# A transform table in four parts, a later first transform, and eleven weight groups fetched ahead, in a one-core convolution and spectral-mixing kernel

## The chip, the cores and the metric

The kernel runs on one core of a Trainium2 chip. The metric is the device time of one execution in microseconds (us), the median of several runs. A core has TensorE (PE; PEld is its weight load), VectorE (DVE), ScalarE (ACT), GpSimd (POOL) and SyncE (SP). Here GpSimd issues the loads of inputs and weights, and SyncE the stores of the output.

## What is computed

A causal convolution of 7 taps along the sequence, with one set of softmaxed taps for each of 8 heads of 24 channels. Its result goes through a Fourier transform along the sequence; the lowest 64 modes are multiplied by a complex 192 x 192 matrix each; the inverse transform is added, and a last product with a clamp follows.

```python
# x (8, 3264, 192), weight (8, 7); B, S, D, H, K, group = 8, 3264, 192, 8, 7, 24
w = np.exp(weight - np.max(weight, axis=-1, keepdims=True))
w = w / (np.sum(w, axis=-1, keepdims=True) + 1e-09)
x_unf = x_pad[:, idx, :].reshape(B, S, K, H, group)
x = np.einsum('hk,bskhg->bshg', w, x_unf).reshape(B, S, D)
# w_r, w_i (64, 192, 192), w_ch (192, 192)
X = np.fft.rfft(x, axis=1)
Xr, Xi = (np.real(X[:, :n_modes]), np.imag(X[:, :n_modes]))
Yr = np.einsum('bmd,mde->bme', Xr, w_r) - np.einsum('bmd,mde->bme', Xi, w_i)
Yi = np.einsum('bmd,mde->bme', Xr, w_i) + np.einsum('bmd,mde->bme', Xi, w_r)
Y[:, :n_modes] = Yr + 1j * Yi
u = x + np.fft.irfft(Y, n=S, axis=1)
out = u + np.maximum(u @ w_ch, 0.0)
```

## The kernel before

Every engine runs its instructions in the order in which the program writes them, so the order of the text is the order of each queue.

**Layout.** The 8 batches are taken as 4 pairs (`q`). Of each batch, 26 tiles of 128 rows lie in `xall` (bf16). The pairs are worked off in units `(q, b0, n)` of n double tiles: pair 0 in three units of 3, 4 and 6, the others in two units of 7 and 6, nine in all. `load_unit` (L144 on) loads a unit from memory by GpSimd, one DMA for each of its two batches (L150) and one for the last, shorter tile (L154). `arena` holds, at first, temporary arrays (`turns`, `whole`, the taps, masks and indices), then five buffers for groups of spectral weights, then the outputs. `ct` (312 blocks of 128 x 128) will hold the transposed `xall`; the blocks of the last pair serve as three more weight buffers before that (`late`). `spots` lists the eight buffers, and `wts` says which group lies in which.

**Head.** VectorE and ScalarE clear arrays, GpSimd makes indices (`cidx`, `sidx`, `midx`, L160 to L165), TensorE multiplies zeros (`NIDLE` times, L180). VectorE makes masks (L184), the softmax runs (L186 to L196, the exponential on ScalarE, L189, and a small sine behind it, L190), and the taps are put into `packed` under masks (L204), in two halves of four heads. Copies of 32 rows each, four for each half, make `band` of it: the first half on ScalarE (L212), the second on VectorE (L214).

**The Fourier table.** `ftab` holds cosines and sines for 26 tiles x 64 modes. `table(step, t0, t1)` makes a part of it in six steps: a product (L223), rounding by a large constant (L226), the difference (L228), on VectorE; the sine (L230), the absolute value (L232) and the cosine (L234), on ScalarE. It is made in two parts, of 14 and 12 tiles: the first part's VectorE steps ahead of unit 0, its ScalarE steps behind it; the whole second part behind unit 1.

**Convolution.** `conv_step` (L294 on) does one head and one parity of a unit with matmuls against `band`: lower rows at once, upper rows two steps later. For pair 0 one PSUM tile of two banks holds both parities of a head; there are four such tiles. The result is copied back over `xall`: L331 on ScalarE, L333 on VectorE, by a rule of head and unit. For the other pairs there are eight tiles of one bank, and L339 (ScalarE) and L341 (VectorE) copy.

**Forward transform.** `dft(q, t0, t1)` (L355) multiplies the tiles of `xall` by `ftab` and sums; the first half of a pair's sum is kept in `xacc` (L358, L360), the second is added to it (L362). `xtrans(q)` (L374, L376) transposes the sum into `xt`, with casts on VectorE (L383) and ScalarE (L385). For pair 0, `dft` over 14 tiles stands behind unit 1, and that over the other 12 and `xtrans` behind unit 2. For the other pairs both are done by `dfts` in the middle of a later unit, after head 2. Six filler matmuls (L421) stand behind unit 0.

**Mixing.** Weights come in 16 groups of four modes, each two DMAs of GpSimd (`load_w`, L273): eight groups after unit 3, others as `mix` frees a buffer. `mix(g)` (L495) multiplies a group; `mix_copy` (L508, L510) scales the result into `ymix` on ScalarE, `mix_trans` transposes it, and two copies (L535, L537) put it into `yet`. Between the mixes `some(n)` takes n jobs of a list of 44: four banks of transposed `ftab`, a small job for `wsw`, and 39 banks of eight transposed blocks of `xall` into `ct` (L456, copied by L446 on ScalarE every third time, else by L448 on VectorE). The two PSUM banks of the mix are cleared by VectorE (L439).

**Output.** From the last mixes on, `both` (L565), `full` (L627) and `product` (L696) make 104 output tiles in PSUM; ScalarE clamps (L620), VectorE adds `xall` (L607), SyncE stores.

Of the kernel before, what the change touches and what calls it, by code (L numbers as in the profile page):

```python
# [9 lines left out]
ALU = mybir.AluOpType  # L10
ACT = mybir.ActivationFunctionType
AX = mybir.AxisListType
F32 = mybir.dt.float32
BF16 = mybir.dt.bfloat16
U16 = mybir.dt.uint16
PSUM = bass.MemoryType.PSUM


@with_exitstack
def kernel(  # L20
# [9 lines left out]
    nc = tc.nc  # L30
# [15 lines left out]
    MAGIC = 12582912.0  # L46
    NIDLE = 31
    UNITS0 = ((0, 3), (3, 4), (7, 6))
# [7 lines left out]

    NW = 5
    WGB = 4 * 3 * D
    sb("pad", [64], BF16)
# [27 lines left out]

    late = ct[:, 3 * NT * (NQ - 1):3 * NT * NQ, :].rearrange("p t s -> p (t s)")
    spots = [arena[:, WGB * i:WGB * (i + 1)] for i in range(NW)]
    spots += [late[:, WGB * i:WGB * (i + 1)] for i in range(3)]  # L90
    spots = [a.rearrange("p (m j e) -> p m j e", m=4, j=3) for a in spots]
    wts = [spots[g] if g < NW + 3 else spots[(g - NW - 3) % NW] for g in range(MODES // 4)]

    zwl = spots[NW - 1].rearrange("p m j e -> p (m j e)").rearrange("p (b t d) -> p b t d", t=2, b=B - 2)
    NO = 6
# [20 lines left out]
    wrec = temp(H, F32)  # L116
    wsin = temp(H, F32)
    cidx = temp(PW, F32)
# [24 lines left out]

    def load_unit(q, b0, n):  # L144
        nf = min(n, NB - 1 - b0)
        s0 = NB * q + b0 + 1
        for i in range(2):
            off = ((2 * q + i) * S + 2 * P * b0) * D
            src = bass.AP(tensor=x.tensor, offset=x.offset + off, ap=[[2 * D, P], [2 * P * D, nf], [1, 2 * D]])
            nc.gpsimd.dma_start(out=xin[:, s0:s0 + nf, 2 * D * i:2 * D * (i + 1)], in_=src)  # L150
        if nf < n:
            off = (2 * q * S + 2 * P * (NB - 1)) * D
            src = bass.AP(tensor=x.tensor, offset=x.offset + off, ap=[[2 * D, PL], [S * D, 2], [1, 2 * D]])
            nc.gpsimd.dma_start(out=xin[0:PL, s0 + nf, :].rearrange("p (i c) -> p i c", i=2), in_=src)  # L154
# [3 lines left out]
                                           ap=[[0, P], [KK, H], [1, KK]]))  # L158
    load_unit(*units[0])
    nc.gpsimd.iota(cidx[:, 0:PW], pattern=[[1, PW]], base=0, channel_multiplier=-1,  # L160
                   allow_small_or_imprecise_dtypes=True)
    load_unit(*units[1])
    nc.gpsimd.iota(sidx.rearrange("p (b a) -> p b a", a=2), pattern=[[2 * P, NB], [1, 2]], base=0,
                   channel_multiplier=2, allow_small_or_imprecise_dtypes=True)
    nc.gpsimd.iota(midx, pattern=[[1, MODES]], base=0, channel_multiplier=0,  # L165
                   allow_small_or_imprecise_dtypes=True)
    nc.vector.memset(packed, 0.0)
    nc.vector.memset(xin[:, 0, :], 0.0)
    bandrow = shared[:, 0:H * 2 * BW]
    nc.scalar.copy(out=bandrow[:, H * BW:], in_=packed[:, 0:1].to_broadcast([P, H * BW]))  # L170
    nc.vector.memset(bandrow[:, 0:H * BW], 0.0)
    for g in range(4):
        nc.vector.memset(goff[32 * g:32 * g + 32, :], float(32 * g))
    nc.vector.memset(xin[PL:P, NB:NB * NQ + 1:NB, :], 0.0)
    nc.vector.memset(halfpi[:], math.pi / 2)
# [7 lines left out]
    for k in range(KK // 2 + 1):  # L183
        nc.vector.tensor_scalar(out=masks[:, PW * k:PW * (k + 1)], in0=cidx[:, 0:PW],  # L184
                                scalar1=float(k), scalar2=None, op0=ALU.is_equal)
    nc.vector.reduce_max(out=wmax, in_=wr3, axis=AX.X)  # L186
    nc.vector.tensor_tensor(out=wsub.rearrange("p (h k) -> p h k", h=H), in0=wr3,
                            in1=wmax.unsqueeze(2).to_broadcast([P, H, KK]), op=ALU.subtract)
    nc.scalar.activation(out=wexp, in_=wsub, func=ACT.Exp)  # L189
    nc.scalar.activation(out=wsin, in_=ascale.to_broadcast([P, H]), func=ACT.Sin)  # L190
    we3 = wexp.rearrange("p (h k) -> p h k", h=H)
# [8 lines left out]
    for h0 in (0, H // 2):  # L200
        hs = slice(h0, h0 + H // 2)
        for lag in range(KK):
            k = lag // 2
            nc.vector.copy_predicated(  # L204
                out=pk4[:, hs, lag % 2, :],
                mask=masks[:, PW * k:PW * (k + 1)].unsqueeze(1).to_broadcast([P, H // 2, PW]),
                data=ta3[:, hs, KK - 1 - lag:KK - lag].to_broadcast([P, H // 2, PW]))
        for g in range(4):
            c0 = 1 + 32 * (g % 2)
            dst, srcv = band[32 * g:32 * g + 32, hs, :, c0:c0 + PW], pk4[32 * g:32 * g + 32, hs, :, :]  # L210
            if h0 == 0:
                nc.scalar.copy(out=dst, in_=srcv)  # L212
            else:
                nc.vector.tensor_copy(out=dst, in_=srcv)  # L214
    nc.vector.tensor_scalar(out=sidx, in0=sidx, scalar1=1.0 / S, scalar2=None, op0=ALU.mult)
    tu3 = turns.rearrange("p (t m) -> p t m", t=NT)
    wh3 = whole.rearrange("p (t m) -> p t m", t=NT)

    def table(step, t0, t1):
        n = t1 - t0  # L220
        tu, wh = tu3[:, t0:t1, :], wh3[:, t0:t1, :]
        if step == 0:
            nc.vector.tensor_tensor(out=tu, in0=sidx[:, t0:t1].unsqueeze(2).to_broadcast([P, n, MODES]),  # L223
                                    in1=midx.unsqueeze(1).to_broadcast([P, n, MODES]), op=ALU.mult)
        elif step == 1:
            nc.vector.tensor_scalar(out=wh, in0=tu, scalar1=MAGIC, scalar2=-MAGIC, op0=ALU.add, op1=ALU.add)  # L226
        elif step == 2:
            nc.vector.tensor_tensor(out=tu, in0=tu, in1=wh, op=ALU.subtract)  # L228
        elif step == 3:
            nc.scalar.activation(out=ftab[:, t0:t1, 1:2 * MODES:2], in_=tu, func=ACT.Sin, scale=-TWOPI)  # L230
        elif step == 4:
            nc.scalar.activation(out=wh, in_=tu, func=ACT.Abs)  # L232
        else:
            nc.scalar.activation(out=ftab[:, t0:t1, 0:2 * MODES - 1:2], in_=wh, func=ACT.Sin, scale=-TWOPI,  # L234
                                 bias=halfpi[:, 0:1])

    load_unit(*units[2])
# [63 lines left out]
    def conv_step(u):  # L301
# [26 lines left out]
        if q == 0:  # L328
            srcv = tile0[:, :, 0:2 * GRP * n].rearrange("p a (b i e) -> p a b i e", b=n, i=2)
            if (h < 5 if b0 == 0 else h > 4 if b0 == units[1][1] else h % 2):  # L330
                nc.scalar.copy(out=dst, in_=srcv)  # L331
            else:
                nc.vector.tensor_copy(out=dst, in_=srcv)  # L333
# [52 lines left out]

    p1, p2 = (0, 14), (14, NT)
    todo = []
# [8 lines left out]

    for step in range(3):
        table(step, *p1)
    for k, u in enumerate(units):  # L400
        for h in range(H):
            for a in range(2):
                conv_step((*u, h, a))
            if k > 3 and h == 2:
                if pend:
                    xtrans(pend.pop(0))
                dfts()
        if k == 3:
            for g in range(NW + 3):
                load_w(g)  # L410
        if u[0]:
            todo.append((u[0], 2 * u[1], 2 * (u[1] + u[2])))
            continue

        flush()
        if k == 0:
            for step in range(3, 6):
                table(step, *p1)
            z = free.pop(0)
            for _ in range(6):  # L420
                nc.tensor.matmul(z[:, 0, :], band[:, 0, 0, 0:P], band[:, 0, 0:1, 0:P].to_broadcast([P, 4, P]), start=True,  # L421
                                 stop=True, skip_group_check=True)
            free.append(z)
        elif k == 1:
            for step in range(6):
                table(step, *p2)
            dft(0, *p1)
        else:
            free[:] = open_psum("left", (1, 1, 1, 1)) + open_psum("right", (1, 1, 1, 1))
            dft(0, *p2)  # L430
            xtrans(0)
    flush()
# [5 lines left out]
    for z in zm:  # L438
        nc.vector.memset(z[:, 0:2 * D], 0.0)  # L439
    tbank = [0]  # L440
    ncopy = [0]

# [47 lines left out]
    def mix(g, bank):  # L490
        yp = bank[:, D * (g % 2):D * (g % 2) + D]
        for j in range(3):
            for p4 in range(4):
# [3 lines left out]
                                 tile_position=(0, 32 * p4), skip_group_check=True)  # L497
        if g < NW:
            load_w(g + NW + 3)
        elif g >= NW + 3:  # L500
            load_w(g + NW)

# [132 lines left out]
    for d in range(ND - 2):  # L635
        mix(2 * d, zm[d % 2])
        mix(2 * d + 1, zm[d % 2])
        mix_copy(d, zm[d % 2], 0, 2)

        some(2 if d < 4 else 4)  # L640
        mix_trans(d, 0, 2)
        some(2 if d < 4 else 4 if d < ND - 3 else 8)
    d = ND - 2
# [15 lines left out]
    zw_pair(2, zm[0], zm[1])  # L659
    zw_pair(3, ze[0], ze[1])  # L660
    mix(NG - 1, zm[0])
    mix_copy(d, zm[0], 1, 1)
    both(1, 0, "c", begin=True)
    mix_trans(d, 1, 1)
    both(1, 1, "c")
    for b in range(2):
# [118 lines left out]
```

## Time and profile before

| | us |
|---|---|
| median of 3 runs (lowest, highest) | 176.38 (176.29, 176.39) |
| profiled execution, its own time | 177.44 |
| span of the profiled execution | 175.6 |

The table below gives busy time by stage, in us, from the windows of the profiled execution; the last column is the rate of all DMA.

| stage, us of the span | PE | DVE | ACT | GB/s |
|---|---|---|---|---|
| 0 to 32.3: head and pair 0 | 27.94 | 22.48 | 17.42 | 177 |
| 32.3 to 72: pairs 1 to 3 | 39.23 | 25.39 | 23.00 | 205 |
| 72 to 77.5: last transform | 4.14 | 3.04 | 1.49 | 199 |
| 77.5 to 113.4: mixing and transposes | 34.54 | 23.70 | 23.00 | 137 |
| 113.4 to 175.6: output | 57.62 | 56.36 | 47.13 | 326 |

A line of the timeline has the start, the duration, engine, line, operation, what is written and read with its shape (partitions x elements), and how many instructions are merged; in brackets stand the engine's idle time before it and what ended that. A line of the windows has the stretch, its length, then busy time and number of instructions of PE, PEld, DVE, ACT and POOL, the granted clock, the share of the DMA engines and GB/s. The granted clock is 0.997 of full speed over the span.

### The profile page before, as it was taken

What the parts mean: (1) busy time and instruction counts of PE and PEld (TensorE: products, weight loads), DVE (VectorE), ACT (ScalarE), POOL (GpSimd) and SP (SyncE); (2) the same over time, 40 slices, a digit from 0 to 9 for tenths busy, and PEclk for the clock granted to TensorE, in tenths of its full rate; (3) what the DMA queues carried; (4) which work ended last, traced back from release to release, by engine and by line L of the source; (5) the groups of instructions that cost most, each with busy time, mean ns of one, the idle gap of its engine ahead of it and who ended that gap; (6) DMA issues with size and microseconds to landing.
All of it is one profiled execution on the core that took longest, in us unless ns stands there. A gap on an engine that the chain in (4) does not pass through costs nothing.

```text
span 175.6 us, 7070 instructions
## 1 busy us (share of the span) xinstructions
PE 163.5 (93%) x2969; PEld 131.0 (75%) x2969; DVE 131.0 (75%) x268; ACT 112.0 (64%) x223; POOL 52.4 (30%) x95
## 2 busy tenths in 40 slices
PE   6999798899999999879998999999999999999990
PEld 2366565678687697659997976499999999999960
DVE  6897763584593593477675964889999999999991
ACT  5458383375384474347775764488788888888870
POOL 7969722423423353019252000386000000000000
PEclk9999999999999999999999999999999999999998
DMA  3999999999999999989999970079999998989996
GB/s 48 175 192 203 204 204 203 204 203 202 205 201 206 206 209 204 207 152 144 203 209 203 207 126 0 26 255 356 371 321 345 343 325 333 356 296 359 364 350 225
DMA packets 37392, 40.15 MB, mean 229 GB/s; under 512 B 2512, under 2 KB 37360, under 8 KB 37360
## 3 DMA queue, kind: packets, MB, share of 16 engines
q0 software_dynamic: 22848, 19.62, 70.3%
q1 hardware_dynamic: 14512, 20.09, 31.4%
q8 instruction: 23, 0.38, 0.9%
q14 instruction: 9, 0.07, 0.1%
HBM read 39.10 MB, written 20.05 MB: 337 GB/s over the span
## 4 chain that ended last, share of the span: by engine, by line
PE 80%; DMA 7%; DVE 6%; ACT 3%; issue 2%; POOL 1%; DVEq 0%; ACTq 0%
PE z L696 33%; PE z L294 18%; PE z L355 9%; PE z L456 7%; DMA arena<-in_moe_w_i_dram 7%; PE z L180 6%; PE z L495 2%; DVE xall L333 1%; DVE xall L341 1%; PE z L574 1%; PE z L374 1%; PE z L627 1%; PE z L421 1%; PE z L575 1%; ACT xall L331 1%
## 5 line engine op out<-in xcount | busy, mean ns | idle before, releaser
L607 DVE TENSOR_TENSOR arena<-z,xall 128x384 f32<-128x384 f32 (+1 forms) x104 | 57.4, 557 | 2.9 <-PE z L696 0.8
L620 ACT ACTIVATE z<-z 128x384 f32<-128x384 f32 x102 | 48.5, 475 | 12.1 <-PE z L696 2.4
L696 PEld LDWEIGHTS <-ct 64*128 64x128 bf16 x600 | 42.4, 94 | 3.7 <-PE z L627 0.6
L696 PE MATMUL z<-arena,ftab 64*128 64x384 bf16 x308 | 44.9, 322 | 0.0
L294 PE MATMUL z<-xall,shared 64*64 64x288 bf16 (+3 forms) x1152 | 39.4, 280 | 1.4 <-DVE xall L333 1.0
L294 PEld LDWEIGHTS <-shared 64*64 64x64 bf16 x1152 | 33.8, 106 | 7.3 <-issue 5.1
L696 PE MATMUL z<-wsw,ct 64*128 64x192 bf16 x300 | 35.1, 243 | 0.0
L696 PEld LDWEIGHTS <-ftab 64*128 64x128 bf16 x396 | 29.7, 93 | 2.7 <-issue 0.5
L341 DVE CAST xall<-z 128x336 bf16<-128x336 f32 (+1 forms) x48 | 23.0, 482 | 11.2 <-PE z L294 8.7
L696 PE MATMUL z<-wm,ct 64*128 64x192 bf16 x200 | 30.0, 243 | 0.0
L339 ACT CAST xall<-z 128x336 bf16<-128x336 f32 (+1 forms) x48 | 20.1, 419 | 10.7 <-PE z L294 6.5
L696 PE MATMUL z<-w,ct 64*128 64x192 bf16 x100 | 24.3, 243 | 0.0
L448 DVE COPY ct<-z 128x1024 bf16<-128x1024 bf16 x26 | 17.2, 686 | 7.0 <-PE z L456 6.6
L456 PE MATMUL z<-ident,xall 128*128 128x128 bf16 x312 | 19.8, 219 | 0.0
L355 PE MATMUL z<-xall,ftab 128*128 128x384 bf16 (+1 forms) x104 | 18.3, 326 | 1.3 <-ACT xall L331 0.7
L150 POOL DMA_DIRECT2D xall<-in_x_dram x18 | 15.8, 887 | 8.9 <-DMA xall<-in_x_dram 8.1
L456 PEld LDWEIGHTS <-xall 128*128 128x128 bf16 x312 | 17.8, 98 | 0.8
L355 PEld LDWEIGHTS <-ftab 128*128 128x128 bf16 (+1 forms) x104 | 9.7, 98 | 8.4 <-issue 1.7
L446 ACT COPY ct<-z 128x1024 bf16<-128x1024 bf16 x13 | 13.2, 1013 | 4.3 <-PE z L456 4.2
L273 POOL DMA_DIRECT2D arena<-in_moe_w_r_dram x13 | 8.1, 621 | 21.1 <-PE z L495 16.1
L696 PE MATMUL z<-mixa,ftab 64*128 64x384 bf16 x88 | 13.6, 323 | 0.0
L522 POOL DMA_DIRECT2D arena<-xs x16 | 7.9, 504 | 18.3 <-ACT xs L518 17.4
(112 smaller groups left out, 149.5 us busy)
## 6 DMA issues: line engine op xcount, KB each, us to landing
out_dram<-arena SPq DMA_DIRECT2D x47, 384.0 KB, 3.8
xall<-in_x_dram POOLq DMA_DIRECT2D x6, 672.0 KB, 16.8
xall<-in_x_dram POOLq DMA_DIRECT2D x8, 480.0 KB, 16.6
arena<-in_moe_w_r_dram POOLq DMA_DIRECT2D x13, 288.0 KB, 10.5
arena<-in_moe_w_i_dram POOLq DMA_DIRECT2D x13, 288.0 KB, 11.2
ct<-in_moe_w_r_dram POOLq DMA_DIRECT2D x3, 288.0 KB, 11.8
ct<-in_moe_w_i_dram POOLq DMA_DIRECT2D x3, 288.0 KB, 11.8
out_dram<-arena SPq DMA_DIRECT2D x3, 288.0 KB, 3.0
```

The costliest lines, as they stand in the source:

```text
L150: nc.gpsimd.dma_start(out=xin[:, s0:s0 + nf, 2 * D * i:2 * D * (i + 1)], in_=src)
L180: nc.tensor.matmul(free[3][:, 0, :], zeros, zeros.unsqueeze(1).to_broadcast([P, 4, P]), start=True, stop=True, skip_group_check=True)
L294: yield nc.tensor.matmul(o, band[r, h, int(a != a1), c0:c0 + 64], xin5[r, s1:s1 + n, :, a1, dsl], start=(row == 0 and a1 == 0), stop=(row ...
L339: nc.scalar.copy(out=dst[:, a], in_=srcv)
L341: nc.vector.tensor_copy(out=dst[:, a], in_=srcv)
L355: nc.tensor.matmul(xp, ftab[0:k, t, :], xall[0:k, NT * q + t, :, :], start=(t == t0), stop=(t == t1 - 1), skip_group_check=True)
L446: nc.scalar.copy(out=out, in_=in_)
L448: nc.vector.tensor_copy(out=out, in_=in_)
L456: nc.tensor.matmul(o, in_, ident[:], start=True, stop=True, is_transpose=True)
L607: nc.vector.tensor_tensor(out=o[0:pn, :, a, :], in0=bank[0:pn, 0:2 * D].rearrange("p (i d) -> p i d", i=2), in1=xall[0:pn, s + a, :, :], o ...
L620: nc.scalar.activation(out=z, in_=z, func=ACT.Relu)
L696: mm = nc.tensor.matmul(target(bank[k], cols, r), l, r, start=first, stop=last, skip_group_check=True)
```

## The change

- The table is made in four parts, of 6, 8, 6 and 6 tiles. The absolute value moves from ScalarE to VectorE, as a mask on the sign bit. The first part's four VectorE steps stand ahead of the softmax, its sine and cosine behind the exponential; the small sine goes. The other parts are spread over units 0 to 2 by `chores`: a key (k, h) names the place behind head h of unit k, or behind the unit.
- Clearing `band` goes to ScalarE as a whole; so does the clearing of the tails of `xall`. Of the eight band copies ScalarE has three. Unit 0's copies back are all on ScalarE, those of units 1 and 2 alternate.
- GpSimd makes its indices behind the first of unit 0's two DMAs.
- 27 idle matmuls in place of 31, two fillers behind unit 1 in place of six behind unit 0.
- Pair 0's first `dft` stands behind unit 2, the second in unit 3 and its `xtrans` in unit 4.
- Eleven groups of weights are fetched after unit 3; `late` takes six buffers at the end of `ct`, and a group's buffer is its number modulo eleven.
- `some(3)` twice in every round of the mix, in place of 2 and 2, later 4 and 4, then 4 and 8.
- The mix's banks are cleared by matmuls with zeros; the count that shares copies between engines starts at 1.
- `both(1, ...)` stands ahead of the last `mix` in place of behind it.

```diff
-    NIDLE = 31
+    NIDLE = 27
...
-    late = ct[:, 3 * NT * (NQ - 1):3 * NT * NQ, :].rearrange("p t s -> p (t s)")
-    spots = [arena[:, WGB * i:WGB * (i + 1)] for i in range(NW)]
-    spots += [late[:, WGB * i:WGB * (i + 1)] for i in range(3)]
+    late = ct[:, 3 * NT * NQ - NL * WGB // P:3 * NT * NQ, :].rearrange("p t s -> p (t s)")
+    spots = [arena[:, WGB * (i % NW):WGB * (i % NW + 1)] for i in range(NW - 1, 2 * NW - 1)]
+    spots += [late[:, WGB * i:WGB * (i + 1)] for i in range(NL)]
...
-    wts = [spots[g] if g < NW + 3 else spots[(g - NW - 3) % NW] for g in range(MODES // 4)]
+    wts = [spots[g % (NW + NL)] for g in range(MODES // 4)]
...
-    load_unit(*units[0])
-    nc.gpsimd.iota(cidx[:, 0:PW], pattern=[[1, PW]], base=0, channel_multiplier=-1,
-                   allow_small_or_imprecise_dtypes=True)
-    load_unit(*units[1])
+    load_unit(*units[0], which=(0,))
...
+    nc.gpsimd.iota(cidx[:, 0:PW], pattern=[[1, PW]], base=0, channel_multiplier=-1,
+                   allow_small_or_imprecise_dtypes=True)
+    load_unit(*units[0], which=(1,))
+    load_unit(*units[1])
...
-    bandrow = shared[:, 0:H * 2 * BW]
-    nc.scalar.copy(out=bandrow[:, H * BW:], in_=packed[:, 0:1].to_broadcast([P, H * BW]))
-    nc.vector.memset(bandrow[:, 0:H * BW], 0.0)
+    zero = packed[:, 0:2].bitcast(F32)
+    bandrow = shared[:, 0:H * 2 * BW].bitcast(F32)
+    nc.scalar.copy(out=bandrow, in_=zero.to_broadcast([P, H * BW]))
...
-    nc.vector.memset(xin[PL:P, NB:NB * NQ + 1:NB, :], 0.0)
+    tails = xin[PL:P, NB:NB * NQ + 1:NB, :].bitcast(F32)
+    nc.scalar.copy(out=tails, in_=zero[PL:P, :].unsqueeze(2).to_broadcast([P - PL, NQ, 2 * D]))
...
+        elif step == 3:
+            nc.vector.tensor_scalar(out=wh.bitcast(U32), in0=tu.bitcast(U32), scalar1=0x7FFFFFFF, scalar2=None,
+                                    op0=ALU.bitwise_and)
+        elif step == 4:
+            nc.scalar.activation(out=ftab[:, t0:t1, 1:2 * MODES:2], in_=tu, func=ACT.Sin, scale=-TWOPI)
...
+    P0, P1, P2, P3 = (0, 6), (6, 14), (14, 20), (20, NT)
+    nc.vector.tensor_scalar(out=sidx, in0=sidx, scalar1=1.0 / S, scalar2=None, op0=ALU.mult)
+    for step in range(4):
+        table(step, *P0)
...
     nc.scalar.activation(out=wexp, in_=wsub, func=ACT.Exp)
-    nc.scalar.activation(out=wsin, in_=ascale.to_broadcast([P, H]), func=ACT.Sin)
+    table(4, *P0)
+    table(5, *P0)
...
-            if h0 == 0:
+            if g == 3 or (g, h0) == (2, 0):
                 nc.scalar.copy(out=dst, in_=srcv)
...
-            if (h < 5 if b0 == 0 else h > 4 if b0 == units[1][1] else h % 2):
+            if b0 == 0 or h % 2:
                 nc.scalar.copy(out=dst, in_=srcv)
...
-    for step in range(3):
-        table(step, *p1)
+    chores = {(0, 0): [(P1, range(4))], (0, 4): [(P2, range(2))], (0, H): [(P1, (4, 5)), (P2, (2, 3))],
+              (1, H): [(P3, range(4)), (P2, (4, 5))], (2, H): [(P3, (4, 5))]}
+
+    def tables(k, h):
+        for part, steps in chores.get((k, h), ()):
+            for step in steps:
+                table(step, *part)
...
-            if k > 3 and h == 2:
+            tables(k, h)
+            if k > 2 and h == 2:
                 if pend:
                     xtrans(pend.pop(0))
                 dfts()
         if k == 3:
-            for g in range(NW + 3):
+            for g in range(NW + NL):
                 load_w(g)
...
         flush()
-        if k == 0:
-            for step in range(3, 6):
-                table(step, *p1)
+        tables(k, H)
+        if k == 1:
             z = free.pop(0)
-            for _ in range(6):
+            for _ in range(2):
...
-        elif k == 1:
-            for step in range(6):
-                table(step, *p2)
-            dft(0, *p1)
-        else:
+        elif k == 2:
             free[:] = open_psum("left", (1, 1, 1, 1)) + open_psum("right", (1, 1, 1, 1))
-            dft(0, *p2)
-            xtrans(0)
+            todo[:] = [(0, 14, NT)]
+            dft(0, 0, 14)
...
-        nc.vector.memset(z[:, 0:2 * D], 0.0)
+        nc.tensor.matmul(z[:, 0:2 * D], w1[0:64, 0:P], w1[0:64, :], start=True, stop=True, skip_group_check=True)
     tbank = [0]
-    ncopy = [0]
+    ncopy = [1]
...
-        if g < NW:
-            load_w(g + NW + 3)
-        elif g >= NW + 3:
-            load_w(g + NW)
+        load_w(g + NW + NL)
...
-        some(2 if d < 4 else 4)
+        some(3)
         mix_trans(d, 0, 2)
-        some(2 if d < 4 else 4 if d < ND - 3 else 8)
+        some(3)
...
+    both(1, 0, "c", begin=True)
+    both(1, 1, "c")
     mix(NG - 1, zm[0])
     mix_copy(d, zm[0], 1, 1)
-    both(1, 0, "c", begin=True)
     mix_trans(d, 1, 1)
-    both(1, 1, "c")
```

## The prediction

> **What bounds the kernel now.** I read the page first (engine shares and the chain that ended last), then the timeline of TensorE, then those of VectorE and ScalarE for the first 34 us, then GpSimd's queue and the DMA rate in 2 us windows.
>
> ```profile
> PE 163.5 (93%) x2969; PEld 131.0 (75%) x2969; DVE 131.0 (75%) x268; ACT 112.0 (64%) x223; POOL 52.4 (30%) x95
> ...
> PE 80%; DMA 7%; DVE 6%; ACT 3%; issue 2%; POOL 1%; DVEq 0%; ACTq 0%
> ```
>
> TensorE sets the end: 80% of the chain. The 7% of DMA (11.46 us, the load of a late weight group) misleads: the chain steps into that load because it landed last, but TensorE worked through nearly all of it. The last line of the next fence (TensorE's timeline) shows what TensorE lost there: 0.78 us.
>
> ```profile
> 1.62 9.74 PE L180 MATMUL z<-xall 128*128 128x512 bf16 x31 [1.62 <-DVE xall L168]
> ...
> 14.41 1.47 PE L421 MATMUL z<-shared 128*128 128x512 bf16 x6
> ...
> 18.41 2.22 PE L294 MATMUL z<-xall,shared 64*64 64x192 bf16 x72 [1.01 <-DVE xall L333]
> ...
> 28.98 2.11 PE L355 MATMUL z<-xall,ftab 128*128 128x384 bf16 x12 [0.73 <-ACT xall L331]
> ...
> 77.53 0.72 PE L495 MATMUL z<-arena,mixa 128*16 128x192 bf16 x24 [1.31 <-ACT ftab L446]
> ...
> 94.23 0.47 PE L495 MATMUL z<-arena,mixa 128*16 128x192 bf16 x12 [0.78 <-DMA arena<-in_moe_w_i_dram]
> ```
>
> So TensorE's losses that an edit can reach are: 9.74 us of idle matmuls, 1.47 of filler, stalls of 1.01, 0.73 and 0.65 us in the first pair, 1.31 ahead of the first mix, 0.78 at a weight load. From 113.4 to 170.0 us the chain stays on it without a gap, beside VectorE at 19.2 of 20 us; nothing is edited there, so a gain ahead of it moves the end one for one.
>
> ```profile
> 2.69 1.34 DVE L174 MEMSET xall<- 32x1536 uint32 x1 [0.27 <-issue]
> ...
> 6.79 3.09 DVE L204 COPY_PREDICATED arena<-arena 128x140 bf16<-128x140 uint16 x14
> 9.91 1.08 DVE L214 COPY shared<-arena 32x280 bf16<-32x280 bf16 x4
> ...
> 11.59 1.09 DVE L223 TENSOR_TENSOR arena<-arena 128x896 f32<-128x896 f32 x1
> 12.72 0.63 DVE L226 TENSOR_SCALAR arena<-arena 128x896 f32<-128x896 f32 x1
> ...
> 20.04 0.95 DVE L223 TENSOR_TENSOR arena<-arena 128x768 f32<-128x768 f32 x1
> 21.02 0.56 DVE L226 TENSOR_SCALAR arena<-arena 128x768 f32<-128x768 f32 x1
> ```
>
> ```profile
> 2.03 1.06 ACT L170 COPY shared<-arena 128x1040 bf16<-128x1040 bf16 x1
> ...
> 5.83 1.28 ACT L190 ACT_TABLE_LOAD   x1
> ...
> 8.41 1.75 ACT L212 COPY shared<-arena 32x280 bf16<-32x280 bf16 x4 [1.07 <-DVE arena L204]
> ...
> 14.51 1.21 ACT L230 ACTIVATE ftab<-arena 128x896 bf16<-128x896 f32 x1 [0.48 <-DVE arena L228]
> ```
>
> These rows, from the timelines of VectorE and ScalarE, price the new order: two sizes of the same table step give cost per element.
>
> ```profile
> 78.30 0.61 POOL L273 DMA_DIRECT2D arena<-in_moe_w_r_dram x1 [9.24 <-PE z L495]
> ```
>
> ```profile
> 78.00:80.00 2.00, 2.00 (x42) 1.73 (x33) 1.28 (x3) 1.41 (x5) 1.70 (x3) 1.00 0.36 47
> ...
> 104.00:106.00 2.00, 1.61 (x29) 0.90 (x28) 0.75 (x2) 0.82 (x3) 0.00 (x0) 1.00 0.09 17
> ```
>
> The first is GpSimd's timeline, the others are two of the 2 us windows, their last column GB/s. The weight stream ran at 205, paused while GpSimd waited 9.24 us for the first mix to free a buffer, and ended near 103.5.
>
> **Prices of the table.** A VectorE product or difference: 1.09 us at 896 elements, 0.95 at 768, so 0.11 + 1.09 ns each: 0.53 at 384, 0.67 at 512. Rounding: 0.63 and 0.56, so 0.35 and 0.42. The new sign mask on VectorE has no row: at least the rounding (0.35 at 384), at most the product (0.53); it is a one-input form like rounding, so I take 0.35, and 0.18 each stays for the range. Four steps with gaps: 1.9 us (six tiles), 2.35 (eight). ScalarE's sines (1.21 and 1.07; cosines 1.31 and 1.16) give 1.35 a pair at six tiles, 1.65 at eight.
>
> **Head, up to the band.** VectorE loses two fills (0.49, 1.34). The tail fill goes to ScalarE: 1536 elements at 1040 per 1.06 us is 1.57 (3.1 to 4.7 us), in time when it idled until 5.57; uncovered it would cost that. GpSimd: the three iotas (0.30, 0.26, 0.20) now stand ahead of the second DMA of unit 0, which is issued 0.76 us later; unit 1's and 2's, behind the same sum as before, move by about 0.2. Unit 0's 0.59 MB were in by about 7 us at the rate shown, three before use, so this costs nothing; with that lead gone, 0.76.
>
> VectorE is free at 2.3, the column index comes at 2.85; index and masks (1.0) to 3.85, scale 0.5 to 4.4, first table quarter to 6.3, max and difference to 6.75. From there to the taps took 1.22 (5.54 to 6.76): 7.95. So the band's chain starts 1.2 us later than before. Half the predicated copies (1.55) to 9.5, two band copies (0.27 each) to 10.05, second half to 11.6, three copies to 12.4. ScalarE: exponential to 7.05, table load to 8.35 (formerly covered by an idle stretch, now ahead of the band copies), first sines to 9.7, two band copies (0.44) to 10.6, a third, waiting for VectorE until 11.6, to 12.05; behind that wait stand all eight evictions of unit 0.
>
> The load's row is 1.28 us, and the next activation began 0.02 after it. The Trainium skill (ScalarE: Activation LUTs, "What ACT_TABLE_LOAD costs") adds a drain of some 1.38 us to every switch; the row here shows none, and with it the upper band would come at 12.0 and the sum be 1.4 us worse.
>
> **TensorE through the first pair.** Idle matmuls end at 1.62 + 27 x 0.314 = 10.1. Lower rows can start then; upper ones wait for 10.6, so the conv runs as if from 10.4 (before: 11.36). Four heads fit the four PSUM tiles; head 4 waits for ScalarE's first eviction, 12.05 + 0.36: 12.45; four heads at 0.39: 14.05. The six fillers go. Unit 1: four heads at 0.47 to 15.95, then the new wait: head 4 needs VectorE's first eviction, which stands behind the second quarter (2.35) and the third's four steps (1.9): 12.4 + 4.25 + 0.5 = 17.2 with the handover, 1.2 us lost. Unit 1 ends at 19.1, two fillers 0.5, unit 2 as before 5.3 to 24.9 (the last quarter, 1.9 on VectorE from 19.4, is done at 21.3, ahead of head 4's need at 22.1), the bank change 0.75, first transform 2.45: 28.1. The second transform (2.13) and its transposes (0.5) move into units 3 and 4, where no eviction bounds TensorE: as work they still count, 2.65. That is 30.75 against 32.28 before: **1.5 us gained**. Bounds: without any stall after 10.1 (3.1 + 3.8 + 0.5 + 5.3 + 0.75 + 2.45 + 2.65) 28.65, gain 3.6; with the mask and rounding at the product's rate and the band 0.9 later besides, about zero.
>
> **Before the first mix.** The two zero fills (0.79 on VectorE) become two matmuls of 0.17. VectorE starts its first copy at 74.9 instead of 75.7, the second copy goes to ScalarE, and the last channel transpose's cast, which ended at 77.44, ends at 76.4; ScalarE's half, behind its 1.01 copy, at 76.7. **Gain 0.75.**
>
> **Weights.** Three more groups are six more issues of 0.61 on GpSimd ahead of the 9.24 wait. A group is 0.59 MB, 2.9 us at 205 GB/s. Group 7 lands near 77.2, so without the pause group 11 lands at 88.8, 13 at 94.6, 15 at 100.4. With six transposed banks in every round (3.7 us), the mixes start at 75.2, 78.9 and so on: group 11 at 94, 13 at 98, 15 near 105. None waits: **gain 0.78**. Three us of slack cover it. The banks only move earlier; their number and the 59 ns per transpose stay. Each late buffer is overwritten by transposes only a round or more after its mix in TensorE's own order, so no new wait.
>
> **Last mix.** Before, the first duo's products (0.42 and 0.37) filled the gaps behind the last mix's eviction and transposes. Now they precede it; TensorE idles for the eviction (107.85 to 108.23, 0.38) and for the two copies (0.37). The weights being early, this hides nothing: **loss 0.75**.
>
> Sum: 1.5 + 0.75 + 0.78 - 0.75 = 2.3. The profiled execution took 177.44 with a span of 175.6, the rest lying around it; the shown median is 176.38. The span should become 173.3, the median **174.1 us**.
>
> **Rivals.**
> - More from the head (20%): VectorE and ScalarE keep ahead, and TensorE runs from 10.1 almost without stall. For it: rows that follow each other on an engine overlap by some hundredths, and ScalarE idled for 6.3 of its first 12.2 us (0.73, 2.48, 1.07, 2.07). Against: VectorE's 4.25 us before unit 1's first eviction. A head gain of 3.1 to 3.6: 172.2.
> - The head gives nothing (12%): slow mask, later band. Only 0.78 remains: 175.6.
> - Slower, the band chain (11%): four table steps, table load and two sines stand ahead of the band. At the 768-element prices (0.95, 0.56, 0.95, 0.95) the steps take 1.5 us more, and were the load to double, ScalarE's band copies and unit 0's evictions come 2.8 later. TensorE waits for all of it, and the point of no gain is an upper band at 12.9 instead of 10.6. 176.9. Against: the two sizes give a clean line.
> - The clock (4%): fewer fillers, a 1.2 us stall. In 17 to 19 us TensorE was busy about half the time and was granted 1.00. Were it halved over unit 1's last four heads, the fillers and two heads of unit 2 (1.9 + 0.5 + 1.3 us), 177.8. The Trainium skill (TensorE: Matmul & The Clock Gate, Part 1) has the clock halve after an idle window of about 3.4 us; the trace's gaps of up to 1.3 kept it, in agreement.
> - The prefetch doesn't help (3%): a later group is waited for as long, and the 0.78 stays: 174.9.
>
> The forecast holds 50%, its own range 173.2 to 175.2 (mask price, unit 1's stall by 0.9 either way). For 8 in 10, from 172.0 to 176.5, which leaves out the slower cases and the head's extreme. About 0.2% (0.35 us) is what a measurement can tell from none. Faster 0.80 (forecast, more from the head, prefetch, two thirds of no head gain), same 0.06, slower 0.14.
>
> **What would show it.** Conv starting near 10.1 to 10.6 and a TensorE wait on VectorE's eviction in unit 1 of about 1.2 us; first transform ended by 28.1; the first mix at 75.2; no TensorE wait on a weight DMA; DMA at 205 GB/s without the dip at 78 to 80; two new gaps of 0.4 behind the last mix; an unchanged 62 us from where the chain enters the output stage (113.4) to the end. Wrong if the upper band comes after 12.9, if a mix waits for a load, or if the stretch behind the mixes changes length.

## The result, and the profile after

The changed kernel takes 179.04 us (178.57 to 179.31) against 176.38: a ratio of 1.0147, 95% interval 1.0123 to 1.0171. It is slower by 2.66 us; the forecast had it faster by 2.3 us.

The page's second part shows the first pair in slices of 4.4 us; the third line is the granted TensorE clock:

```profile
span 176.7 us, 7069 instructions
...
PE   6956798999999999899999988999999999999980
...
PEclk9999699999999999999999999999999999999999
```

TensorE's timeline of the changed kernel (start, duration, what, idle before it):

```profile
10.22 1.46 PE L303 MATMUL z<-xall,shared 64*64 64x144 bf16 x56 [0.87 <-DVE shared L245]
12.65 3.18 PE L303 MATMUL z<-xall,shared 64*64 64x144 bf16 x128 [0.96 <-ACT xall L340]
17.29 0.44 PE L303 MATMUL z<-xall,shared 64*64 64x192 bf16 x10 [1.46 <-DVE xall L342]
19.04 3.10 PE L303 MATMUL z<-xall,shared 64*64 64x192 bf16 x62 [1.32 <-issue]
22.07 0.67 PE L436 MATMUL z<-shared 128*128 128x512 bf16 x2
...
28.36 2.44 PE L364 MATMUL z<-xall,ftab 128*128 128x384 bf16 x14 [0.73 <-ACT xall L340]
...
75.18 0.50 PE L451 MATMUL z<-w 64*128 64x384 bf16 x2
...
78.16 0.71 PE L507 MATMUL z<-arena,mixa 128*16 128x192 bf16 x24 [0.35 <-ACT mixa L394]
...
108.69 0.29 PE L468 MATMUL z<-ident,shared 128*128 128x128 bf16 x2 [0.44 <-ACT shared L519]
109.27 0.30 PE L583 MATMUL z<-wm,yet 128*128 128x192 bf16 x1 [0.30 <-DVE yet L544]
```

The second line merges unit 0's last 72 matmuls and unit 1's first 56. The conv starts 1.07 us sooner than before; the four PSUM tiles (the wait of 0.96 us for ScalarE's first copy back) and VectorE's late copy back (1.46 us) stop it as forecast; then, up to 19.04, comes a wait of 1.32 us that has no releaser, and 62 matmuls take 3.10 us. The windows of the changed kernel show that those ran at half the clock (the last three columns are the clock, DMA share and GB/s):

```profile
16.00:17.00 1.00, 0.00 (x0) 0.00 (x0) 0.97 (x3) 0.73 (x2) 1.00 (x3) 1.00 1.33 213
...
19.00:20.00 1.00, 0.96 (x25) 0.95 (x28) 0.00 (x0) 0.38 (x1) 0.95 (x2) 0.50 1.31 204
```

One profile of each was not enough: that of before had taken 1.06 us more than its median. Profiled twice more, the kernels stand like this (us of the span at which a matmul of TensorE starts, and the span; unit 6 by its fifth matmul; three profiles of each, the first ones first):

```
                        before                    changed               mean difference
unit 6, fifth matmul    50.40  50.07  50.38       51.45  51.29  51.01     +0.97
first mix               77.53  77.21  77.52       78.16  78.00  77.71     +0.54
mix of group 14        104.02 102.80 103.08      103.64 103.47 103.19     +0.13
first output product   109.63 108.41 108.68      110.09 109.92 109.64     +0.98
last output product    170.10 168.87 169.44      170.83 170.66 170.38     +1.15
span                   175.64 174.38 175.32      176.71 176.96 176.51     +1.61
```

> The kernel before, unchanged, profiled again. If the first profiled execution lay 1.06 us above its median by chance, this one has a span nearer to 174.6, and the stage that is shorter tells where the kernel before scatters. If profiling itself adds it, the span is again about 175.6.

> The kernel before, unchanged, profiled a third time, for the scatter by stage: the end of unit 1's stall, the first mix, the end of TensorE's work and what lies behind it.

> The changed kernel, unchanged, profiled again. If its first profiled execution was a lucky one (176.7 of 176.7 to 177.5), this has a span of 177 or more, and the added time lies in the first pair: a later end of unit 1's stall, or a halved clock for longer than 3.41 us. If the added time lies behind the first mix, the first pair is not what the medians show.

> The changed kernel, unchanged, profiled a third time, for the scatter by stage: the end of unit 1's stall, the halved clock, the first mix, the end of TensorE's work.

They took 176.19 and 177.09 (before), 178.72 and 178.28 us (changed). The changed kernel's three profiles agree within 0.5 us at every stage. The scatter of before lies at the mixes: in the other two profiles no mix waits for a load, and the stretch from the first mix to group 14 is 25.6 us instead of 26.5. By these six, 1.61 of the 2.66 us have a place; the other 1.0 us were not found in a trace.

### The profile page after: what moved, and what is told of

It reads as the page before. It is cut to its first block, busy times and chain, and to the rows that moved or that the text cites. A ratio compares the mean times of both kernels' runs of the same rounds, so it can differ in the third digit from the quotient of the medians.

```text
span 176.7 us, 7069 instructions
## 1 busy us (share of the span) xinstructions
PE 162.4 (92%) x2963; PEld 131.7 (75%) x2963; DVE 130.4 (74%) x271; ACT 112.7 (64%) x228; POOL 52.3 (30%) x95
## 4 chain that ended last, share of the span: by engine, by line
PE 81%; DVE 11%; issue 3%; ACT 2%; POOL 1%; DVEq 0%; POOLq 0%; ACTq 0%
PE z L704 33%; PE z L303 18%; PE z L468 11%; PE z L364 10%; PE z L507 3%; DVE arena L235 2%; DVE xall L350 1%; DVE arena L202 1%; DVE arena L197 1%; PE z L636 1%; PE z L583 1%; PE z L574 1%; PE z L584 1%; PE z L383 1%; DVE xall L342 1%
## 5 line engine op out<-in xcount | busy, mean ns | idle before, releaser
L629 ACT ACTIVATE z<-z 128x384 f32<-128x384 f32 x102 | 48.4, 475 | 12.5 <-PE z L704 2.9
L303 PE MATMUL z<-xall,shared 64*64 64x288 bf16 (+3 forms) x1152 | 40.5, 286 | 4.8 <-DVE xall L342 1.6
L303 PEld LDWEIGHTS <-shared 64*64 64x64 bf16 x1152 | 35.4, 110 | 10.2 <-issue 7.8
L460 DVE COPY ct<-z 128x1024 bf16<-128x1024 bf16 x26 | 17.8, 688 | 5.7 <-PE z L468 5.0
L151 POOL DMA_DIRECT2D xall<-in_x_dram x18 | 15.9, 897 | 10.6 <-DMA xall<-in_x_dram 9.8
L340 ACT CAST xall<-z 128x288 bf16<-128x288 f32 (+2 forms) x16 | 7.1, 481 | 6.5 <-PE z L303 6.5
```

The lines of the kernel that those rows point to most:

```text
L303: yield nc.tensor.matmul(o, band[r, h, int(a != a1), c0:c0 + 64], xin5[r, s1:s1 + n, :, a1, dsl], start=(row == 0 and a1 == 0), stop=(row ...
L460: nc.vector.tensor_copy(out=out, in_=in_)
L629: nc.scalar.activation(out=z, in_=z, func=ACT.Relu)
```

## The experiments

**What TensorE waits for in unit 1.** In the first profile of before the wait at 18.41 was put down to VectorE's copy. The theory that the change suggested instead: TensorE waits for its own code, the next block of its instructions, which DMA brings, at a fixed instruction. Before, 31 idle matmuls, 128 of unit 0, 6 fillers and 56 of unit 1 precede the wait: 221. In the changed kernel it is 27 + 128 + 66: 221 again. Two kernels move the place.

```diff
-    for _ in range(NIDLE):
-        nc.tensor.matmul(free[3][:, 0, :], zeros, zeros.unsqueeze(1).to_broadcast([P, 4, P]), start=True, stop=True,
+    for _ in range(2 * NIDLE):
+        nc.tensor.matmul(free[3][:, 0, 0:2 * P], zeros, zeros.unsqueeze(1).to_broadcast([P, 2, P]), start=True, stop=True,
```

> The kernel before with 62 idle matmuls of 256 columns in place of 31 of 512: the same idle time, 31 more matmuls. If the stall waits for code, it stays before matmul 221 of TensorE's own count, which is now 31 matmuls earlier in unit 1 (its 25th instead of its 56th), and ends 2.2 to 2.4 us after the start of a 16 KB code transfer. If it waits for VectorE, it stays at the 56th matmul of unit 1 and ends at 18.4. The time is within 0.5 us of before by both.

The ratio was 1.0009 (0.9981 to 1.0038). TensorE's timeline of this kernel:

```profile
14.39 1.47 PE L421 MATMUL z<-shared 128*128 128x512 bf16 x6
15.79 0.94 PE L294 MATMUL z<-xall,shared 64*64 64x192 bf16 x25
18.30 3.05 PE L294 MATMUL z<-xall,shared 64*64 64x192 bf16 x103 [1.58 <-issue]
```

62 + 128 + 6 + 25 is 221: the wait moved behind the 25th matmul of unit 1, where TensorE needs no copy of unit 1 yet and VectorE's copies of unit 0 had ended at 15.29. It is code.

```diff
         if k == 0:
             for step in range(3, 6):
                 table(step, *p1)
-            z = free.pop(0)
-            for _ in range(6):
-                nc.tensor.matmul(z[:, 0, :], band[:, 0, 0, 0:P], band[:, 0, 0:1, 0:P].to_broadcast([P, 4, P]), start=True,
-                                 stop=True, skip_group_check=True)
-            free.append(z)
```

> The kernel before without its six filler matmuls behind unit 0, a part of the change alone. If TensorE's stall near 18 us waits for code, it meets it sooner but resumes at the same time: the time stays within 0.3 us of before, or rises where the longer idle time halves the clock, and the stall stands before matmul 221 of TensorE's own count (six later in unit 1). If the stall waits for VectorE's copies back, as the prediction read it, the pair is done about 1.4 us sooner: 175.0.

The ratio was 1.0026 (0.9995 to 1.0056): nothing gained.

```profile
14.62 1.64 PE L294 MATMUL z<-xall,shared 64*64 64x192 bf16 x54 [0.97 <-DVE xall L333]
17.41 2.01 PE L294 MATMUL z<-xall,shared 64*64 64x192 bf16 x66 [1.15 <-issue]
...
37.73 0.77 PE L294 MATMUL z<-xall,shared 64*64 64x288 bf16 x17 [0.70 <-issue]
```

31 + 128 + 62 is 221 again. The expectation missed by 1.0 us where the wait ends: with the conv begun at 10.15 (11.29 before) the code came at 17.41. Unit 3 still began at 31.26, that is 0.6 to 0.9 us sooner than in before's three profiles. Most of this was spent at 37.73 on another late block of code, three blocks on; unit 4 ended at 43.96 us, against 43.76 to 44.14 before.

The trace's DMA records hold the code transfers, 16 KB each (us):

```
kernel                   transfer starts   TensorE resumes   next transfer starts
before                        16.15             18.41               22.12
changed                       16.65             19.04               22.79
before, halved idle           15.92             18.30               21.96
before, no fillers            15.10             17.41               21.14
changed, six fillers          17.11             19.53               23.20
changed, quarter later        16.64             19.07               22.65
```

In these six, TensorE resumes 2.3 to 2.4 us after the start, and the next transfer starts 3.6 to 3.8 us after that, at half the clock and at full. In all 19 profiles the 222nd matmul starts 2.2 to 2.5 us after the start of such a transfer, behind a wait of 0.3 to 2.8 us. In three of them TensorE waits ahead of the 350th too, and gets there 5.9 to 6.1 us after the 222nd (24.94 less 19.07 with the quarter later, below); 128 conv matmuls take as little as 3.2. The Trainium skill (Runtime: NRT & Kernel Launch, "Instruction fetch mechanics") says that code comes in blocks of 16 KiB or 256 instructions, fetched ahead, and that crossing a block is mostly hidden. The block agrees with the transfers' size and with waits 128 matmuls apart (221 and 349, each with its weight load); hidden it was not: here it cost 0.3 to 2.8 us. By that size TensorE's 2969 matmuls with their weight loads are 23 blocks, and the page of before's profile counts 23 such transfers.

**The halved clock and VectorE's late copy.** The clock was half from 18.8 to 22.3 us in all three profiles of the changed kernel. Two edits tell clock, copy and code apart: fillers that keep TensorE busy, and a table that leaves VectorE free.

```diff
-        if k == 1:
+        if k == 0:
             z = free.pop(0)
-            for _ in range(2):
+            for _ in range(6):
```

> The changed kernel, with six filler matmuls behind unit 0 (as before the change) in place of two behind unit 1. They fill time in which TensorE waits for VectorE anyway (its first copy back of unit 1). If the halved clock is what makes the changed kernel slow, and TensorE's idleness behind unit 0 is what halves it, the clock stays full, unit 1 runs at the pace of before and the time falls by 1.3 us or more, to 177.7 or less. If the stalls alone cost the time and the clock is a by-product, unit 1 ends no sooner and the time stays within 0.3 us of 179.0.

The ratio was 1.0106 (1.0077 to 1.0136), some 0.7 us below the change's, with intervals that overlap. The profile still had half a clock for 3.41 us, and TensorE resumed at 19.53. The first expectation fails, and these intervals don't decide the second; by the trace, code stops TensorE with or without fillers.

```diff
-    chores = {(0, 0): [(P1, range(4))], (0, 4): [(P2, range(2))], (0, H): [(P1, (4, 5)), (P2, (2, 3))],
-              (1, H): [(P3, range(4)), (P2, (4, 5))], (2, H): [(P3, (4, 5))]}
+    chores = {(0, 0): [(P1, range(4))], (0, H): [(P1, (4, 5))], (1, H): [(P2, range(4))],
+              (2, H): [(P2, (4, 5)), (P3, range(4))], (3, 1): [(P3, (4, 5))]}
```

> The changed kernel, with the third table part's VectorE steps behind unit 1 and its sines behind unit 2, the fourth part's behind unit 2 and into unit 3. VectorE's first copy back of unit 1 then stands 1.9 us earlier. If TensorE's wait of 1.46 us for that copy and the halved clock behind it are the cause, both go: 2 us or more less, 177.0 or below. If the halved clock comes from the other wait in unit 1 (1.32 us, with no releaser in the profile), only up to 1.4 us goes: 177.6 to 178.5. If the first pair isn't the place, nothing changes.

The ratio was 1.0138 (1.0105 to 1.0172), that of the change. The timeline, then a window:

```profile
12.64 3.67 PE L303 MATMUL z<-xall,shared 64*64 64x144 bf16 x138 [0.68 <-ACT xall L340]
19.07 1.86 PE L303 MATMUL z<-xall,shared 64*64 64x192 bf16 x62 [2.76 <-issue]
...
24.94 2.28 PE L303 MATMUL z<-xall,shared 64*64 64x288 bf16 x62 [0.44 <-issue]
```

```profile
19.00:20.00 1.00, 0.93 (x39) 0.80 (x38) 0.20 (x1) 0.48 (x1) 1.00 (x2) 1.00 1.31 203
```

The wait for VectorE is gone, the clock is full, and TensorE resumes at 19.07, as in the changed kernel. The 1.24 us that the full clock saves in unit 1 (62 matmuls in 1.86 instead of 3.10) are lost at the next block and at other waits: unit 3 begins 0.29 us sooner, unit 4 at 37.46 against 37.49. Neither the copy nor the clock sets the end of the first pair in these profiles. By its time alone this is the third case expected; the trace shows that the pair is the place all the same. What halves the clock is not settled: a wait of 2.76 us left it full here, while with the head alone (next) it was halved at 17.68, behind a single wait of 1.75.

> The changed kernel's first pair alone: weights, first mix and last mix as before the change. If the loss sits in the first pair (TensorE's code for unit 1 arriving near 19 us, and a halved clock behind the idle time), it is about 2 us slower than before (178.5 on the scale of the shown median), with the place between units 3 and 6 about 1 us later than before in the trace. If the loss sits behind the mixes, it is within 0.5 us of before or faster.

This was the changed kernel with the edits of weights, first mix and last mix undone. Ratio 1.0134 (1.0081 to 1.0187), as the first expectation has it; but unit 6 began only 0.5 us later than before's mean, where 1 was expected. Its profiled span (175.7) is the shortest of its six (up to 179.3, at mean clocks of 0.960 to 0.985 against 0.987). The same with six fillers:

> The changed kernel's first pair alone, as tried, with six fillers behind unit 0 in place of two behind unit 1. If the halved clock makes the timed runs slower than the profiled one says (2.4 us against 0.1), the fillers keep the clock and the ratio falls from 1.013 to about 1.005. If the clock does not matter, it stays at 1.013.

It gave 1.0114 (1.0078 to 1.015), no sign of 1.005, and its profile had the full clock up to 175 us. The clock as the main cause of the timed runs' loss falls with it; what they lose beyond the profiles stays open.

**The last mix.** The first duo's products moved back in the changed kernel, and moved ahead in the kernel before:

```diff
+    both(1, 0, "c", begin=True)
+    both(1, 1, "c")
     mix(NG - 1, zm[0])
     mix_copy(d, zm[0], 1, 1)
-    both(1, 0, "c", begin=True)
     mix_trans(d, 1, 1)
-    both(1, 1, "c")
```

> The changed kernel, with the first duo's products behind the last mix again. If their place costs what the two new gaps show (0.44 and 0.30 us of TensorE idle), the time falls by 0.7 to 0.8 us, from 179.0 to about 178.3, and the gaps go. If the output stage, bound by VectorE, takes up the earlier start, the time stays at 179.0.

> The kernel before, with the first duo's products ahead of the last mix and nothing else of the change. By the prediction's sum 0.75 us slower, by the gaps of the changed kernel's trace 0.84. If the output stage takes it up, 0.

The first gave 1.0111 (1.0064 to 1.0159), 0.6 us below the change with intervals that overlap, the second 1.0077 (1.0048 to 1.0105), 1.4 us above before. TensorE's timeline of before, then that of the second:

```profile
107.73 0.26 PE L565 MATMUL z<-wm,ct 64*128 64x192 bf16 x2
...
108.23 0.28 PE L456 MATMUL z<-ident,shared 128*128 128x128 bf16 x2
108.45 0.26 PE L565 MATMUL z<-wm,ct 64*128 64x192 bf16 x2
```

```profile
108.52 0.28 PE L456 MATMUL z<-ident,shared 128*128 128x128 bf16 x2 [0.43 <-ACT shared L510]
109.10 0.30 PE L574 MATMUL z<-wm,yet 128*128 128x192 bf16 x1 [0.30 <-DVE yet L535]
```

The two gaps are those of the changed kernel, and from group 14's mix to the first output product this kernel needs 6.46 us, before 5.61; the changed kernel needs 6.45, and with the products moved back 5.61 again. The products (L565) had covered them. So the traces show 0.85 us; the timed 1.4 has that within its interval.

**The weights.** Before with the eleven groups and six jobs a round, as in the change's diff:

> The kernel before, with the eleven weight groups fetched ahead and three jobs twice in every round, and nothing else of the change. As in the prediction: the wait for a weight load (0.78 us) goes and nothing takes its place: 175.6 against 176.38. A rival: the banks of transposes taken earlier only move the wait, and the time stays at 176.4.

The ratio was 0.9982 (0.9955 to 1.001), which includes no gain at all. No mix waits for a load and DMA runs without the dip; but neither do the second and third profiles of before show such a wait. First mix to group 14 takes 25.4 us, against their 25.6.

**Versions.** With the weights in, the rest was tried on the kernel before; in the first, with 28 idle matmuls and the first mix's edits; in the second, the same without the six fillers; in the second, third and fourth, pair 0's transposes stand in unit 3:

```diff
-            if k > 3 and h == 2:
+            if k > 2 and h == 2:
...
-            xtrans(0)
+            pend.append(0)
```

> The kernel before with the eleven weight groups, the first mix's edits (zero matmuls, the copies' count) and 28 idle matmuls in place of 31. By the trace of the weights alone 0.94 us at the end of TensorE's work, by the changed kernel's trace 0.4 at the first mix, and up to 0.8 from a conv that starts 0.85 sooner, if the code for unit 1 is asked for that much sooner: about 174.4 on the scale of the shown median, that is a ratio of 0.989. Without the head's part 0.992.

> The same, without the six fillers and with pair 0's last transposes in unit 3. If code is the limit, unit 1's stall ends near 17 us, and the later stall that ate this up in the kernel without fillers (0.70 us near 37.7, code again, asked for late because TensorE sat waiting for the first pair's sum) goes, since nothing waits there: another 0.6 to 1.0 us off, a ratio of 0.985. If the idle time halves the clock, it is slower than the one with fillers.

> The kernel before with the eleven weight groups (0.998 alone) and pair 0's last transposes in unit 3, with its 31 idle matmuls and six fillers. TensorE's wait for the first pair's sum (0.65 us at 31.1 to 31.7) goes, and the code behind it is asked for sooner: 0.6 us less than with the weights alone, a ratio of 0.995. If unit 3's code is the limit there, nothing is gained: 0.998.

> The same with the first mix's edits. If the zero matmuls find their bank free, as in the changed kernel, another 0.4 us: a ratio of 0.992. If they wait for the last sum's bank, as in the kernel before with these edits (0.72 us), it is 0.3 us slower than without them.

The first gave 1.0054 (1.0026 to 1.0081), a miss. Its timeline has a new wait ahead of the zero matmuls:

```profile
75.16 0.48 PE L440 MATMUL z<-w 64*128 64x384 bf16 x2 [0.72 <-DVE xs L363]
```

In this order of PSUM banks VectorE probably still reads the last sum from the bank to be cleared; in the changed kernel the zero matmuls (75.18) wait for nothing. The second gave 0.9999 (0.9976 to 1.0022): its code came at 18.06, not 17. The third gave 0.9974 (0.995 to 0.9998), 176.07 us beside 176.72 of before: faster than before by some 0.5 us, half of what was expected, with an interval that all but reaches none. The fourth, with the first mix's edits, gave 0.9985 (0.9957 to 1.0013): these edits add nothing there.

## Why the prediction was wrong, point by point

- **The step that failed: "TensorE through the first pair", 1.5 us gained; measured 0.97 us lost** at unit 6. The first transform was to end at 28.1 and ended at 30.7. Its starts were right (conv as if from 10.4, measured 10.22; head 4 at 12.45, measured 12.65; a wait of 1.2 us for VectorE in unit 1, measured 1.46, and 0.75 ahead of the first transform, measured 0.73). It counted the stall of before at 18.41, as a wait on VectorE, and the fillers among the losses that an edit can reach. The halved idle shows that stall to be code, and the kernel without fillers that they only stood in front of it. All that was saved ahead of matmul 221 was waited away there, and the code itself came some 0.6 us later (transfers at 15.8 to 16.2 us in before's three profiles, 16.3 to 16.7 in the changed kernel's). Why it came later stays open. One block ahead, the 94th matmul starts at 12.6 to 12.8 us in before's profiles and at 12.5 to 12.8 in the changed kernel's: the conv's earlier start is gone by then, but TensorE is no later there. And with the head alone changed, the same instructions so far, the transfer started at 16.20.
- **The rival "the clock"** (4%, 3.7 us lost) happened in part: the clock was halved, though with six fillers it was halved too in one of two profiles, so fewer fillers are not shown to be its cause. Its price was wrong: in the profiles 1.24 us in unit 1, 0.3 of it left at unit 3. The forecast took the trace's full clock through gaps of 1.3 us as a reason against it; here two gaps fell into the 3.41 us ahead of 18.82, where it was halved.
- **The rival "the band chain"** (11%) had the sign but not the mechanism: the upper band was there by 10.6, far from 12.9.
- **Weights: 0.78 forecast, 0.2 to 0.3 found.** The load's wait did go, but the size came from a wait that only that profiled execution had. The prediction put the 1.06 us between this execution and the median aside as a constant. Part of it was this wait: the second profile, without it, is 1.25 us shorter, 0.9 of that between first mix and group 14; the third, also without it, is only 0.35 us shorter, as it loses time behind the last product.
- **First mix: 0.75 forecast, 0.43 found**; ScalarE's half releases the mix, as forecast (it ended 0.06 us ahead). But the two zero matmuls took 0.50 us, not 0.34, and in the first profiles the first transposes stand 0.52 us further behind the start of the last transform than before.
- **Last mix: a loss of 0.75 forecast, 0.85 found.** Right, for the reason given.
- **"An unchanged 62 us" behind it**: 0.17 us more to the last product, and 0.46 behind that, where the stores end and each kernel's three profiles scatter by 0.4; not explained.

The sum of the steps as measured is 0.97 - 0.43 - 0.41 + 0.85 + 0.17 + 0.46 = 1.61 (the 0.41 with the first profile's wait in it).

## What to carry to other kernels

A stall that stands at the same instruction count in several versions, a fixed time behind a code transfer, is code, whatever releaser the profile names: count the instructions ahead of it before a gain is booked there. Fillers in front of it cost nothing here (1.0026 without them). Where the profiled execution is slower than the median, look in it for a wait that the others may not have; profile again before pricing it. Work that stands between a product and its consumers is cover, and moving it forward for its own sake opens the gaps that it filled.

## What the hardware showed that was not expected

Where TensorE waited for two blocks of code in a row, the second reached it 5.9 to 6.1 us after it had entered the first; ahead of the 222nd matmul it stood for 0.3 to 2.8 us. The clock was halved for 3.41 us after a stretch of 3.41 us (15.4 to 18.8) in which TensorE was busy for 0.86 us; it was not idle throughout. The Trainium skill (TensorE: Matmul & The Clock Gate, Part 1) names an idle window of that length as the cause; the length agrees, and a quarter of a window's work did not prevent it. Nor did about half: with the head alone it was busy for 1.66 of the 3.41 us ahead of the halved clock, with six fillers for 1.60.
